# Reading the moving operand of the large products one column from each half in turn

## The chip, the core and the metric

The kernel runs on one core of a Trainium2 chip, a single program with one launch. The metric is device time in microseconds. Each of the kernel's large products is a TensorE instruction that streams a moving operand of 128 partitions x 512 columns past a stationary one of 128 x 128 and adds into an accumulator of 512 fp32 columns.

## The reference

Linear attention over q, k and v of shape (8, 8, 576, 64) gives 4608 tokens of 512 values. Two feed-forward layers of width 2048 follow, the first with ELU between its products, the second with a rational function. Some inputs are scaled by 8, weights come partly as float64 (by their bits).

```python
q_s = softmax(q, over d); k_s = softmax(k, over s)
kv = einsum('bhsd,bhse->bhde', k_s, v)
x = einsum('bhsd,bhde->bhse', q_s, kv)        # then tokens x 512
h = x @ w_in;  g = where(h > 0, h, exp(min(h, 0)) - 1);  x = g @ w_out
h = x @ w2_in
g = (a0 + a1*h + a2*h**2 + a3*h**3) / (1 + |b0|*|h| + |b1|*h**2 + 1e-6)
out = g @ w2_out
```

## The kernel before

Tokens are worked in 9 blocks of 512 (`TB`). Inside a block, position i*128 + p of a tile holds token 4p + i, since the attention loads rows four to a partition. A product in full precision is made of three TensorE products of fp32r halves: high x high, high x low, low x high. Weights lie in slots as high and low halves, inputs as tiles `xs` and `gs` (or `g`) of 128 x 2 x 512, high and low.

`plan_in` makes one tile of h (128 hidden columns x 512 tokens): for 4 pieces of the 512 inputs, three products each (lines 632 to 634), with the weights `w_in` stationary and the tokens `xs` moving, into a PSUM bank `ps`. `plan_elu` and `plan_rational` turn h into g element by element on ScalarE, VectorE and GpSimd (line 203 makes the high half, line 206 the low). `plan_out` multiplies g by `w_out` at line 673 into four accumulators `acc`: in the first layer `w_out` is stationary and the tokens g move, so the result has tokens along the columns again; in the second layer g is stationary and `w_out` moves, so the result has 128 tokens on the partitions. A tile takes 12 products in and 12 out; there are 2 layers x 9 blocks x 16 tiles, 6912 large products in all. `plan_store` copies each finished accumulator to an SBUF tile `e` (ScalarE, line 711; for the two first blocks, whose sums are made in two halves, VectorE adds at line 707) and stores it (line 715). The result's rows go out four apart, as the tokens lie.

Beside it the attention runs, one block ahead: fp32 products at lines 501 and 558 and transposes at lines 479, 486 and 547. At the start the weights of the first layer are made from float64 bits on VectorE and ScalarE (lines 317 to 362).

The order of all instructions is set by `Plan.run`: every piece of work has engines with a cost in us, what it comes after, a rank and the buffers that it takes and frees; the planner lets simulated time run and issues what can start first, lower rank first. Three large products have the cost 0.68 there (lines 645 and 683), a copy on ScalarE 0.62. Each engine works its instructions in the order issued.

Of the kernel before, what the change touches and what calls it, by code (L numbers as in the profile page):

```python
# [12 lines left out]
AF = mybir.ActivationFunctionType  # L13
ALU = mybir.AluOpType
# [4 lines left out]
P = 128  # L19
TB = 512  # L20
# [3 lines left out]
class Plan:  # L24
# [15 lines left out]
    def op(self, engines, fn, after=(), rank=0.0, take=(), free=(), extra=0.0, follow=()):  # L40
        o = dict(follow=[a for a in follow if a is not None], issued=None, engines=engines, fn=fn, after=[a for a in after if a is not None], rank=rank, take=take,
                 free=free, extra=extra, held={}, end=None, next=[], n=len(self.ops))
        waits = o["after"] + o["follow"]
        o["left"] = len(waits)
        for a in waits:
            a["next"].append(o)
        self.ops.append(o)
        return o
# [55 lines left out]
def linear_attention_elu_rational(  # L104
# [31 lines left out]
    nc = tc.nc  # L136
# [4 lines left out]
    KD = DM // P  # L141
# [13 lines left out]
    x1_d = {(j, i): dram.tile([P, TB], F32, name=f"x1_{j}_{i}") for j in range(NB) for i in range(KD)}  # L155
# [17 lines left out]
    op = plan.op  # L173

    def PE(c):
        return (("PE", c),)
# [4 lines left out]
    def DVE(c=0.75):  # L181
        return (("DVE", c),)

    def ACT(c=0.62):
        return (("ACT", c),)
# [10 lines left out]
    def f32_tile(tag, bufs, pool=None):  # L196
        return (pool or main).tile([P, TB], F32, tag=tag, name=tag, bufs=bufs)

    def bank():
        return ps_p.tile([P, TB], F32, tag="ps", name="ps")  # L200

    def copy_hi(hi, src):
        nc.scalar.activation(out=hi, in_=src, func=AF.Copy)  # L203
# [202 lines left out]
    last = {}  # L406
# [11 lines left out]
    def plan_pair(j, hp, r, gate=None):  # L418
# [58 lines left out]
        def k_maxT(e):  # L477
            b["mt"] = bank()
            nc.tensor.transpose(b["mt"][:, 0:P], b["km"].rearrange("p h d -> p (h d)"), ident)
# [17 lines left out]
        def kv_mm(e):  # L497
            pk = b["pk"] = bank()
            for i in range(NS):
                for h in range(2):  # L500
                    nc.tensor.matmul(pk[h * D:(h + 1) * D, 0:D + 1], b["ke"][:, i, h], b["vt"][:, i, h],  # L501
                                     start=(i == 0), stop=(i == NS - 1))
# [41 lines left out]
        def q_T(e):  # L544
            pt = b["pt"] = bank()
            for i in range(4):
                nc.tensor.transpose(pt[:, i * P:(i + 1) * P], b["qe"][:, i].rearrange("p h d -> p (h d)"), ident)  # L547
# [60 lines left out]
    slot_ready = {}  # L608
# [9 lines left out]
    def step_of(L, j, f):  # L618
        return place[L, j, f]

    def plan_in(t, b):
        L, j, f = t
        s = step_of(*t)

        def mm(kks):
            def fn(e):
                if 0 in kks:
                    b["h"] = bank()
                w = slot[f, 0].rearrange("p s (k c) -> p s k c", c=P)
                for kk in kks:  # L630
                    x = x_tile[L, j, kk]
                    nc.tensor.matmul(b["h"], w[:, 0, kk, :], x[:, 0], start=(kk == 0), stop=False)  # L632
                    nc.tensor.matmul(b["h"], w[:, 0, kk, :], x[:, 1], start=False, stop=False)  # L633
                    nc.tensor.matmul(b["h"], w[:, 1, kk, :], x[:, 0], start=False, stop=(kk == KD - 1))  # L634
            return fn

        parts = [(i,) for i in range(KD)] if f in (0, KF - 1) else [tuple(range(KD))]
        o = None
        for n, kks in enumerate(parts):
            free = []  # L640
            if f == KF - 1:
                free += [(x_owner[L, j, kk][0], x_owner[L, j, kk][1]) for kk in kks]
            if j == NB - 1 and n == len(parts) - 1 and f % 2:
                free.append((f"w{f // 2}_0", slot_owner[L, f, 0]))
            o = op(PE(0.68 * len(kks)), mm(kks),
                   [last.get("mm_in"), slot_ready[L, f, 0]] + [x_ready[L, j, kk] for kk in kks],
                   s, take=["bank"] if n == 0 else [], free=free,
                   follow=[x_owner[L, j, kk][1] for kk in range(KD)] if n == 0 and f == 0 else [])
            if n == 0:
                b["h_op"] = o  # L650
            last["mm_in"] = o
        in_ops[t] = o
        return o

    def plan_out(t, b):
        L, j, f = t
        halves = L == 0 and j < 2
        f0, f1 = (f - f % HALF, f - f % HALF + HALF - 1) if halves else (0, KF - 1)
        r = step_of(*t) + (1.2 if step_of(*t) < HALF else LAG[L] + 0.5)

        def mm(idx):
            def fn(e):
                for i in idx:
                    if f == f0:
                        accs[L, j, i] = acc_p.tile([P, TB], F32, tag="acc", name="acc")
                    o, g, w = accs[L, j, i], b["g"], slot[f, 1]
                    c = slice(i * P, (i + 1) * P)
                    if L == 0:
                        l3 = ((w[:, 0, c], g[:, 0]), (w[:, 0, c], g[:, 1]), (w[:, 1, c], g[:, 0]))
                    else:  # L670
                        l3 = ((g[:, 0, c], w[:, 0]), (g[:, 0, c], w[:, 1]), (g[:, 1, c], w[:, 0]))
                    for n, (lhsT, rhs) in enumerate(l3):
                        nc.tensor.matmul(o, lhsT, rhs, start=(f == f0 and n == 0), stop=(f == f1 and n == 2))  # L673
            return fn

        parts = [(i,) for i in range(4)] if f in (f0, f1) else [(0, 1, 2, 3)]
        for n, idx in enumerate(parts):
            free = []
            if n == len(parts) - 1:
                free.append(b["g_free"])  # L680
                if j == NB - 1 and f % 2:
                    free.append((f"w{f // 2}_1", slot_owner[L, f, 1]))
            o = op(PE(0.68 * len(idx)), mm(idx), [last.get("mm_out"), b["g_op"], slot_ready[L, f, 1]], r,
                   take=["acc"] * len(idx) if f == f0 else [], free=free)
            last["mm_out"] = o
            if f == f0:
                acc_op[L, j, idx[0]] = o
            if f == f1:
                plan_store(L, j, idx[0], o, r + 0.1, halves and (1 if f < HALF else 2))
        out_ops[t] = o  # L690

    accs = {}
# [3 lines left out]
    part_d = {(j, i): dram.tile([P, TB], F32, name=f"part_{j}_{i}") for j in range(2) for i in range(KD)}  # L696
    parts_stored = {}

    def plan_store(L, j, i, o, r, half):
        b = {}  # L700

        def load(e):
            b["e"] = f32_tile("e", 4)
            nc.sync.dma_start(out=b["e"], in_=part_d[j, i])

        def add(e):
            nc.vector.tensor_tensor(out=b["e"], in0=b["e"], in1=accs[L, j, i], op=ALU.add)

        def copy(e):
            b["e"] = f32_tile("e", 4)  # L710
            nc.scalar.activation(out=b["e"], in_=accs[L, j, i], func=AF.Copy)

        def store(e):
            dst = part_d[j, i] if half == 1 else x1_d[j, i] if L == 0 else out[j * TB:(j + 1) * TB, :].rearrange("(p i) c -> p i c", i=4)[:, i, :]
            nc.sync.dma_start(out=dst, in_=b["e"])

        free = [("acc", acc_op[L, j, i])]
        if half == 2:
            l = op(SP, load, [parts_stored[j, i], in_ops[0, j, KF - 1]], r - 1, take=["e"], extra=DMA)
            o1 = op(DVE(), add, [l, o], r, free=free)  # L720
        else:
            l = o1 = op(ACT(), copy, [o], r, take=["e"], free=free)
        o = op(SP, store, [o1], r, extra=DMA, free=[("e", l)])
        if half == 1:
            parts_stored[j, i] = o
        else:
            stored[L, j, i] = o
# [31 lines left out]
    def plan_rational(t):  # L759
# [49 lines left out]
        def lo(e):  # L809
            sub_lo(e, b["g"][:, 1], b["p"], b["g"][:, 0])  # L810

        o = plan_in(t, b)
        p1 = op(ACT(0.8), pstart, [o, late_op], s + 0.5, take=["p"])
        o1 = op(ACT(0.69), square, [p1], s + 0.52, take=["s"])
# [30 lines left out]
    for n in range(2 * KF):  # L845
        f, which = divmod(n, 2)
# [10 lines left out]
    for f in range(KF):  # L857
        for which in range(2):
            b = {}
            r = step_of(0, NB - 1, f) + (0.9, 3.0)[which]  # L860
# [52 lines left out]
    with tc.manual_schedule():  # L913
# [29 lines left out]
        o = op(SP, load_ab, [in_ops[0, 1, 0]], 0.0)  # L943
        op(ACT(0.2), minus_a, [o, in_ops[0, 2, 0]], 0.0)
        o = op(ACT(0.2), abs_b1, [o, in_ops[0, 2, 0]], 0.0)
        o = op(DVE(0.1), seed_b1, [o], 0.0)
        for _ in range(3):
            o = op(DVE(0.5), heron, [o], 0.0)
# [29 lines left out]
```

## Time and profile before

| | us |
|---|---|
| median of 3 runs | 1720.69 (1720.66 to 1720.9) |
| span of the profiled execution | 1719.4 |
| TensorE busy | 1676.2 |
| VectorE busy | 1065.4 |
| ScalarE busy | 1012.7 |
| GpSimd busy | 818.4 |

The profiled execution took 1719.4 us from its first to its last instruction; its own time is the span plus what lies around the span, and the median of the runs is 1.3 us over the span. The mean granted clock of TensorE is 0.992. TensorE's busy time must be read with care: a large product shows a duration of about 390 ns, but the next one starts long before it ends, so the distance of the starts is what counts. In the chain of waits each step lasts until the next one starts.

### The profile page before, as it was taken

What the parts mean: (1) busy time and instruction counts of PE and PEld (TensorE: products, weight loads), DVE (VectorE), ACT (ScalarE), POOL (GpSimd) and SP (SyncE); (2) the same over time, 40 slices, a digit from 0 to 9 for tenths busy, and PEclk for the clock granted to TensorE, in tenths of its full rate; (3) what the DMA queues carried; (4) which work ended last, traced back from release to release, by engine and by line L of the source; (5) the groups of instructions that cost most, each with busy time, mean ns of one, the idle gap of its engine ahead of it and who ended that gap; (6) DMA issues with size and microseconds to landing.
All of it is one profiled execution on the core that took longest, in us unless ns stands there. A gap on an engine that the chain in (4) does not pass through costs nothing.

```text
span 1719.4 us, 21897 instructions
## 1 busy us (share of the span) xinstructions
PE 1676.2 (97%) x7888; PEld 1363.7 (79%) x7888; DVE 1065.4 (62%) x1504; ACT 1012.7 (59%) x1696; POOL 818.4 (48%) x616
## 2 busy tenths in 40 slices
PE   4899999999999999999999999999999999999999
PEld 2577878888888887888888788888888888888887
DVE  7998646454444444422123777776868686868686
ACT  4565535454444445434456777676768686868675
POOL 2233424333333333323465756565747474747554
PEclk8899999999999999999999999999999999999999
DMA  8712433323322323210233001000101010101000
GB/s 271 231 45 81 136 114 101 90 94 90 106 72 68 114 73 117 63 43 7 92 98 104 19 15 35 13 31 2 48 1 50 1 50 0 50 0 38 0 25 25
DMA packets 110925, 112.58 MB, mean 65 GB/s; under 512 B 48864, under 2 KB 82656, under 8 KB 110816
## 3 DMA queue, kind: packets, MB, share of 16 engines
q1 hardware_dynamic: 106016, 110.00, 20.3%
q10 hardware_dynamic: 4800, 1.18, 0.3%
q8 instruction: 62, 1.02, 0.2%
q14 instruction: 47, 0.39, 0.1%
HBM read 81.79 MB, written 29.36 MB: 65 GB/s over the span
## 4 chain that ended last, share of the span: by engine, by line
PE 90%; DVE 4%; DMA 2%; ACT 1%; issue 1%; POOL 1%; SPq 0%; ACTq 0%; POOLq 0%; DVEq 0%
PE acc L673 44%; PE ps L632 14%; PE ps L634 14%; PE ps L633 14%; PE ps L558 2%; PE ps L501 1%; DMA bits<-in_moe_w_out_dram 1%; PE ps L547 1%; POOL gs L206 1%; DMA bits<-in_moe_w_in_dram 1%; DVE s L786 0%; DVE x L329 0%; DVE m L789 0%; DVE x L320 0%; DVE bits L342 0%
## 5 line engine op out<-in xcount | busy, mean ns | idle before, releaser
L632 PE MATMUL ps<-xs,w_in 128*128 128x512 f32 x1152 | 458.0, 398 | 2.8 <-DVE p L795 2.7
L634 PE MATMUL ps<-xs,w_in 128*128 128x512 f32 x1152 | 450.6, 391 | 0.0
L633 PE MATMUL ps<-xs,w_in 128*128 128x512 f32 x1152 | 449.5, 390 | 0.0
L673 PE MATMUL acc<-gs,w_out 128*128 128x512 f32 x1728 | 435.1, 397 | 4.6 <-POOL gs L206 4.6
L673 PEld LDWEIGHTS acc<-gs,w_out 128*128 128x128 f32 x1728 | 319.3, 188 | 78.1 <-POOL gs L206 7.2
L206 POOL TENSOR_TENSOR gs<-m,gs 128x512 fp32r<-128x512 f32 x124 | 168.3, 1358 | 347.0 <-ACT gs L203 290.3
L741 DVE SCALAR_TENSOR_TENSOR m<-m,ps 128x512 f32<-128x512 f32 x144 | 98.6, 685 | 268.7 <-ACT m L738 266.0
L632 PEld LDWEIGHTS ps<-xs,w_in 128*128 128x128 f32 x1152 | 217.3, 189 | 51.4 <-DVE p L795 4.1
L634 PEld LDWEIGHTS ps<-xs,w_in 128*128 128x128 f32 x1152 | 217.0, 188 | 46.5
L633 PEld LDWEIGHTS ps<-xs,w_in 128*128 128x128 f32 x1152 | 217.5, 189 | 45.0 <-issue 0.5
L777 POOL TENSOR_TENSOR s<-s,m 128x512 f32<-128x512 f32 x144 | 218.7, 1519 | 32.5 <-ACT m L766 32.5
L673 PE MATMUL acc<-w_out,g 128*128 128x512 f32 x864 | 211.6, 389 | 0.0
L673 PE MATMUL acc<-w_out,gs 128*128 128x512 f32 x864 | 210.5, 389 | 0.0
L735 ACT ACTIVATE m<-ps 128x512 f32<-128x512 f32 x144 | 85.8, 596 | 207.6 <-PE ps L634 175.3
L673 PEld LDWEIGHTS acc<-w_out,g 128*128 128x128 f32 x864 | 162.1, 188 | 33.9 <-DVE g L206 0.3
L673 PEld LDWEIGHTS acc<-w_out,gs 128*128 128x128 f32 x864 | 162.2, 188 | 33.6
L206 POOL TENSOR_TENSOR g<-p,g 128x512 fp32r<-128x512 f32 x71 | 105.1, 1481 | 171.9 <-ACT g L203 109.2
L786 DVE SCALAR_TENSOR_TENSOR s<-s,m 128x512 f32<-128x512 f32 x144 | 148.1, 1028 | 48.9 <-ACT m L783 34.5
L203 ACT ACTIVATE gs<-m 128x512 fp32r<-128x512 f32 x144 | 90.6, 629 | 148.4 <-PE acc L673 124.2
L774 ACT ACTIVATE p<-ps,a_sb 128x512 f32<-128x512 f32 x144 | 112.2, 779 | 108.3 <-PE ps L634 49.3
L792 DVE TENSOR_TENSOR p<-p,ps 128x512 f32<-128x512 f32 x144 | 98.1, 681 | 83.9 <-ACT s L770 75.2
L795 DVE SCALAR_TENSOR_TENSOR p<-p,a_sb,ps 128x512 f32<-128x512 f32 x144 | 107.3, 745 | 62.6 <-ACT m L766 62.3
(102 smaller groups left out, 2016.0 us busy)
## 6 DMA issues: line engine op xcount, KB each, us to landing
x<-e SPq DMA_DIRECT2D x36, 256.0 KB, 2.1
e<-x SPq DMA_DIRECT2D x36, 256.0 KB, 2.8
out_dram<-e SPq DMA_DIRECT2D x36, 256.0 KB, 2.6
kt<-in_k_dram SPq DMA_DIRECT2D x32, 256.0 KB, 2.8
bits<-in_moe_w_in_dram SPq DMA_DIRECT2D x16, 512.0 KB, 7.5
bits<-in_moe_w_out_dram SPq DMA_DIRECT2D x16, 512.0 KB, 7.9
st<-in_moe_w_in_dram SPq DMA_DIRECT2D x16, 512.0 KB, 4.2
w<-x SPq DMA_DIRECT2D x32, 256.0 KB, 2.0
```

The source lines that it names most:

```text
L203: nc.scalar.activation(out=hi, in_=src, func=AF.Copy)
L206: engine[e].tensor_tensor(out=lo, in0=src, in1=hi.bitcast(F32), op=ALU.subtract)
L632: nc.tensor.matmul(b["h"], w[:, 0, kk, :], x[:, 0], start=(kk == 0), stop=False)
L633: nc.tensor.matmul(b["h"], w[:, 0, kk, :], x[:, 1], start=False, stop=False)
L634: nc.tensor.matmul(b["h"], w[:, 1, kk, :], x[:, 0], start=False, stop=(kk == KD - 1))
L673: nc.tensor.matmul(o, lhsT, rhs, start=(f == f0 and n == 0), stop=(f == f1 and n == 2))
L741: nc.vector.scalar_tensor_tensor(out=b["m"], in0=b["m"], scalar=-1.0, in1=b["h"], op0=ALU.add, op1=ALU.max)
L774: nc.scalar.activation(out=b["p"], in_=b["h"], func=AF.Identity, scale=a_sb[:, 3:4], bias=a_sb[:, 2:3])
L777: engine[e].tensor_tensor(out=b["s"], in0=b["s"], in1=b["a"], op=ALU.add)
L786: nc.vector.scalar_tensor_tensor(out=b["s"], in0=b["s"], scalar=1.0 + 1e-6, in1=b["a"], op0=ALU.add, op1=ALU.mult)
L792: nc.vector.tensor_tensor(out=b["p"], in0=b["p"], in1=b["h"], op=ALU.mult)
L795: nc.vector.scalar_tensor_tensor(out=b["p"], in0=b["p"], scalar=a_sb[:, 1:2], in1=b["h"], op0=ALU.add, op1=ALU.mult)
```

## The change

All large products read the moving operand through `two`: from the 512 columns, one column of the first half and one of the second in turn (0, 256, 1, 257, ...). The accumulator is written in plain order; `turned` only gives it the same shape, so column 2c + h holds what column h*256 + c of the moving operand makes. In the first layer this order is taken twice between input and result; the copy at the end reads the accumulator through `back` (every second column, then the others) and so undoes the second of the two turns, and the first stays in the order of the tokens. In the second layer the tokens are turned once more in `plan_in`, after which they lie in their natural order; `w_out`, which moves there, is turned, and the copy turns its columns back. With natural order the result's stores write 128 neighbouring rows each. The copies' destination and the sum of line 707 are split into halves to match. The planner's cost of three large products becomes 0.65. The numbers of instructions of each engine do not change, apart from the planner's order.

```diff
@@ -199,6 +199,18 @@
     def bank():
         return ps_p.tile([P, TB], F32, tag="ps", name="ps")
 
+    def two(ap):
+        return ap.rearrange("p (h c) -> p c h", h=2)
+
+    def turned(ap):
+        return ap.rearrange("p (c h) -> p c h", h=2)
+
+    def halves_of(ap):
+        return ap.rearrange("p (h c) -> p h c", h=2)
+
+    def back(ps):
+        return ps.rearrange("p (c h) -> p h c", h=2)
+
     def copy_hi(hi, src):
         nc.scalar.activation(out=hi, in_=src, func=AF.Copy)
 
@@ -629,9 +641,10 @@
                 w = slot[f, 0].rearrange("p s (k c) -> p s k c", c=P)
                 for kk in kks:
                     x = x_tile[L, j, kk]
-                    nc.tensor.matmul(b["h"], w[:, 0, kk, :], x[:, 0], start=(kk == 0), stop=False)
-                    nc.tensor.matmul(b["h"], w[:, 0, kk, :], x[:, 1], start=False, stop=False)
-                    nc.tensor.matmul(b["h"], w[:, 1, kk, :], x[:, 0], start=False, stop=(kk == KD - 1))
+                    o = turned(b["h"])
+                    nc.tensor.matmul(o, w[:, 0, kk, :], two(x[:, 0]), start=(kk == 0), stop=False)
+                    nc.tensor.matmul(o, w[:, 0, kk, :], two(x[:, 1]), start=False, stop=False)
+                    nc.tensor.matmul(o, w[:, 1, kk, :], two(x[:, 0]), start=False, stop=(kk == KD - 1))
             return fn
 
         parts = [(i,) for i in range(KD)] if f in (0, KF - 1) else [tuple(range(KD))]
@@ -642,7 +655,7 @@
                 free += [(x_owner[L, j, kk][0], x_owner[L, j, kk][1]) for kk in kks]
             if j == NB - 1 and n == len(parts) - 1 and f % 2:
                 free.append((f"w{f // 2}_0", slot_owner[L, f, 0]))
-            o = op(PE(0.68 * len(kks)), mm(kks),
+            o = op(PE(0.65 * len(kks)), mm(kks),
                    [last.get("mm_in"), slot_ready[L, f, 0]] + [x_ready[L, j, kk] for kk in kks],
                    s, take=["bank"] if n == 0 else [], free=free,
                    follow=[x_owner[L, j, kk][1] for kk in range(KD)] if n == 0 and f == 0 else [])
@@ -670,7 +683,7 @@
                     else:
                         l3 = ((g[:, 0, c], w[:, 0]), (g[:, 0, c], w[:, 1]), (g[:, 1, c], w[:, 0]))
                     for n, (lhsT, rhs) in enumerate(l3):
-                        nc.tensor.matmul(o, lhsT, rhs, start=(f == f0 and n == 0), stop=(f == f1 and n == 2))
+                        nc.tensor.matmul(turned(o), lhsT, two(rhs), start=(f == f0 and n == 0), stop=(f == f1 and n == 2))
             return fn
 
         parts = [(i,) for i in range(4)] if f in (f0, f1) else [(0, 1, 2, 3)]
@@ -680,7 +693,7 @@
                 free.append(b["g_free"])
                 if j == NB - 1 and f % 2:
                     free.append((f"w{f // 2}_1", slot_owner[L, f, 1]))
-            o = op(PE(0.68 * len(idx)), mm(idx), [last.get("mm_out"), b["g_op"], slot_ready[L, f, 1]], r,
+            o = op(PE(0.65 * len(idx)), mm(idx), [last.get("mm_out"), b["g_op"], slot_ready[L, f, 1]], r,
                    take=["acc"] * len(idx) if f == f0 else [], free=free)
             last["mm_out"] = o
             if f == f0:
@@ -704,14 +717,15 @@
             nc.sync.dma_start(out=b["e"], in_=part_d[j, i])
 
         def add(e):
-            nc.vector.tensor_tensor(out=b["e"], in0=b["e"], in1=accs[L, j, i], op=ALU.add)
+            e = halves_of(b["e"])
+            nc.vector.tensor_tensor(out=e, in0=e, in1=back(accs[L, j, i]), op=ALU.add)
 
         def copy(e):
             b["e"] = f32_tile("e", 4)
-            nc.scalar.activation(out=b["e"], in_=accs[L, j, i], func=AF.Copy)
+            nc.scalar.activation(out=halves_of(b["e"]), in_=back(accs[L, j, i]), func=AF.Copy)
 
         def store(e):
-            dst = part_d[j, i] if half == 1 else x1_d[j, i] if L == 0 else out[j * TB:(j + 1) * TB, :].rearrange("(p i) c -> p i c", i=4)[:, i, :]
+            dst = part_d[j, i] if half == 1 else x1_d[j, i] if L == 0 else out[j * TB + i * P:j * TB + (i + 1) * P, :]
             nc.sync.dma_start(out=dst, in_=b["e"])
 
         free = [("acc", acc_op[L, j, i])]
```

The cost changes the order in several places. TensorE near 138 us of the span, in the first layer, where a long row of output products stands between two groups of input products (`km` and `top` are the attention's maxima, of which `ident` makes transposes). Before:

```order
L632 MATMUL ps<-xs,w_in 128x512
L633 MATMUL ps<-xs,w_in 128x512
L634 MATMUL ps<-xs,w_in 128x512
L673 MATMUL acc<-gs,w_out 128x512 x39
L479 MATMUL ps<-ident,km 128x128
L673 MATMUL acc<-gs,w_out 128x512 x12
```

After:

```order
L645 MATMUL ps<-xs,w_in 128x512
L646 MATMUL ps<-xs,w_in 128x512
L647 MATMUL ps<-xs,w_in 128x512
L686 MATMUL acc<-gs,w_out 128x512 x12
L491 MATMUL ps<-ident,km 128x128
L686 MATMUL acc<-gs,w_out 128x512 x36
L498 MATMUL ps<-ident,top 128x128
L686 MATMUL acc<-gs,w_out 128x512 x12
```

The first transpose moved ahead of three tiles of output products, and the second one came in before the next input products.

ScalarE at the end of a block in the second layer, with the four copies out of the accumulators (`e<-acc`) between the steps of the rational function (`m`, `s`, `p`) and the next block's halves (`xs`). Before:

```order
L711 ACTIVATE e<-acc 128x512 x2
L203 ACTIVATE xs<-e 128x512
L774 ACTIVATE p<-ps,a_sb 128x512
L780 ACTIVATE m<-s,qbias 128x512
L203 ACTIVATE g_9911<-p 128x512
L783 ACTIVATE m<-m 128x512
L770 ACTIVATE s<-ps,b_sb 128x512
L203 ACTIVATE xs<-e 128x512
L766 ACTIVATE m<-ps,b_sb 128x512
L774 ACTIVATE p<-ps,a_sb 128x512
L203 ACTIVATE xs<-e 128x512
L711 ACTIVATE e<-acc 128x512 x2
```

After:

```order
L725 ACTIVATE e<-acc 128x512
L215 ACTIVATE xs<-e 128x512
L215 ACTIVATE gs<-p 128x512
L780 ACTIVATE m<-ps,b_sb 128x512
L725 ACTIVATE e<-acc 128x512 x2
L215 ACTIVATE xs<-e 128x512
L788 ACTIVATE p<-ps,a_sb 128x512
L215 ACTIVATE g_9939<-p 128x512
L794 ACTIVATE m<-s,qbias 128x512
L784 ACTIVATE s<-ps,b_sb 128x512
L725 ACTIVATE e<-acc 128x512
```

The four copies stand one, two and one now, over about the same number of other steps. On TensorE the twelve products of the block's last tile stand there as three and nine, where before they stood as four times three with input products between.

SyncE's queue in the second layer, loads of a later block's rows (`e<-x`) and stores of the result (`out_dram<-e`). Before:

```order
L890 DMA e<-x_4_0_117 128x512
L890 DMA e<-x_4_1_118 128x512
L715 DMA out_dram<-e 128x512 x2
L890 DMA e<-x_4_2_119 128x512
L890 DMA e<-x_4_3_120 128x512
L715 DMA out_dram<-e 128x512 x2
```

After:

```order
L904 DMA e<-x_4_0_117 128x512
L904 DMA e<-x_4_1_118 128x512
L904 DMA e<-x_4_2_119 128x512
L904 DMA e<-x_4_3_120 128x512
L729 DMA out_dram<-e 128x512 x4
```

All four stores of a block moved behind all four loads.

## Rows read from the trace of the kernel before

**Rows 1.** The page, busy time, share of the span and instructions of each engine:

```profile
PE 1676.2 (97%) x7888; PEld 1363.7 (79%) x7888; DVE 1065.4 (62%) x1504; ACT 1012.7 (59%) x1696; POOL 818.4 (48%) x616
```

**Rows 2.** Stretches in us: length, busy us (instructions) per engine, granted clock, DMA:

```profile
0.00:168.00 168.00, 132.36 (x668) 99.42 (x669) 148.56 (x222) 92.22 (x141) 54.66 (x46) 0.93 0.51 158
168.00:430.00 262.00, 261.57 (x1337) 211.74 (x1336) 141.08 (x243) 121.74 (x215) 97.23 (x85) 1.00 0.34 105
...
830.00:1000.00 170.00, 167.93 (x740) 138.43 (x739) 75.70 (x91) 107.92 (x183) 104.18 (x75) 1.00 0.25 76
1000.00:1300.00 300.00, 299.23 (x1321) 247.52 (x1320) 223.22 (x274) 215.71 (x359) 182.21 (x125) 1.00 0.08 26
1300.00:1600.00 300.00, 300.00 (x1325) 248.51 (x1324) 225.03 (x280) 217.70 (x362) 184.71 (x126) 1.00 0.07 22
```

**Rows 3.** Chain of waits near 140 us: start us, us, engine, tile, line:

```profile
137.02 1.24 DVE km L475
...
138.93 3.71 POOL qt L524
...
146.37 0.84 ACT x L238
...
148.00 1.71 POOL gs L206
149.75 2.77 PE acc L673 x11
```

**Rows 4.** Chain of waits at the end of the span:

```profile
1701.34 13.79 PE acc L673 x60
...
1715.16 0.60 ACT e L711
```

**Rows 5.** Chain of waits from 1000 to 1010 us:

```profile
999.88 2.72 PE acc L673 x12
1002.60 0.23 PE ps L632
...
1003.28 2.72 PE acc L673 x12
1006.00 0.23 PE ps L632
...
1009.40 0.68 PE acc L673 x3
```

**Rows 6.** TensorE by line and shape after 168 us: count, busy us, mean ns, idle before:

```profile
L632 PE MATMUL ps<-xs,w_in 128*128 128x512 f32 x1076 | 425.6, 396 | 2.8 <-DVE p L795 2.7
L634 PE MATMUL ps<-xs,w_in 128*128 128x512 f32 x1077 | 420.1, 390 | 0.0
L633 PE MATMUL ps<-xs,w_in 128*128 128x512 f32 x1077 | 419.1, 389 | 0.0
L673 PE MATMUL acc<-gs,w_out 128*128 128x512 f32 x1545 | 386.5, 396 | 0.4 <-POOL gs L206 0.4
L673 PE MATMUL acc<-w_out,g 128*128 128x512 f32 x864 | 211.6, 389 | 0.0
L673 PE MATMUL acc<-w_out,gs 128*128 128x512 f32 x864 | 210.5, 389 | 0.0
...
L547 PE MATMUL ps<-ident,qe 128*128 128x128 f32 x108 | 16.2, 273 | 0.0
...
L558 PE MATMUL ps<-qT,kvd 128*128 128x256 f32 x16 | 4.1, 378 | 0.0
```

**Rows 7.** Timeline of TensorE: start us, us until the last ends, count:

```profile
442.50 1.02 PE L558 MATMUL ps<-qT,kvd 128*128 128x256 f32 x4
...
157.97 0.60 PE L547 MATMUL ps<-ident,qe 128*128 128x128 f32 x4
```

**Rows 8.** Groups by line and shape, whole span: count, busy us, mean ns, idle before:

```profile
L711 ACT ACTIVATE e<-acc 128x512 f32<-128x512 f32 x72 | 41.6, 594 | 28.9 <-PE acc L673 28.3
...
L475 DVE TENSOR_REDUCE km<-kt 128x128 f32<-128x640 f32 x32 | 41.4, 1295 | 2.3 <-DMA kt<-in_k_dram 2.3
...
L533 DVE TENSOR_REDUCE sm<-qe 128x8 f32<-128x512 f32 x36 | 24.6, 682 | 13.0 <-ACT qe L529 12.9
...
L707 DVE TENSOR_TENSOR e<-e,acc 128x512 f32<-128x512 f32 x8 | 5.5, 683 | 3.1 <-PE acc L673 3.1
```

**Rows 9.** DMA issues: count, KB each, median us to landing:

```profile
x<-e SPq DMA_DIRECT2D x36, 256.0 KB, 2.1
...
out_dram<-e SPq DMA_DIRECT2D x36, 256.0 KB, 2.6
```

## The prediction

> **What bounds the kernel now.** I read the page's busy times first. The line to look at is TensorE: busy 97% of a span of 1719.4 us, while VectorE, ScalarE and GpSimd stand at 62%, 59% and 48% [rows 1]. A mean hides stages, so the second view is busy time by stretch [rows 2]. Up to 168 us TensorE is busy for 132.4 us only, and VectorE for 148.6 of the 168: there the fp32 weights are still being made out of their bits, and the chain of waits near 140 us runs through VectorE, ScalarE and GpSimd lines, not through TensorE [rows 3]. [...]
>
> **The distance.** In the chain of waits a step lasts until the next one starts, so it gives the distance of the starts: 12 products of line 673 from 999.88 us on take 2.72 us, and up to 1009.40 us there are 24 of line 673 and 18 of lines 632 to 634, 42 in 9.52 us, 226.7 ns each [rows 5]. [...]
>
> [...]
>
> **The change part by part.** (1) The address order. The count of products stays at 6912, with the same weights; accumulators are still written in consecutive order. [...] I take the larger of the two overheads seen, 213.3 + 2.3 = 215.6 ns, since the transposes are nearer in kind (weights loaded for each short product). That is 11.1 ns less for each.
>
> How many of them are on the path: after 168 us there are 1076 + 1077 + 1077 + 1545 + 864 + 864 = 6503 [rows 6], so 6503 x 11.1 ns = 72.2 us. The 409 before 168 us would save 4.5 us more, which I put at nothing: their cover is VectorE's conversion of weights. If that cover were thinner than I read it, the 4.5 us come on top.
>
> [...]
>
> (2) The copies out of the accumulators. 72 copies on ScalarE (594 ns) and 8 sums on VectorE (683 ns) now read every second column [rows 8]. No row of before reads an accumulator in steps. Nearest is the reduction of line 475, which hops 64 columns between elements: 1295 / 640 = 2.02 ns an element against 682 / 512 = 1.33 for the plain one of line 533 [rows 8]. That bounds the price by 0.69 x 512 = 0.35 us a copy, 25 us of ScalarE in all, which has 82 us to spare in a stretch of 300 [rows 2]; the bound below is nothing, or a few ns less. I take nothing, since the step here is one column and not 64. On the path lies the last copy (0.35 us at most), and the freeing of accumulators where one block of 512 tokens follows another. There three products take 0.65 us and a copy 0.59, so a copy of 0.94 us would hold TensorE for up to 3 x 0.29 = 0.9 us at each of the 17 such places, 15 us at the very worst.
>
> (3) The stores. The 36 stores of the result move the same 256 KB, to 128 rows in one piece. They land in 2.6 us now, the intermediate stores, already in one piece, in 2.1 [rows 9]. Only the last is on the path: 0 to 0.5 us gained. I take 0.
>
> (4) The order of work. The planner's price of three products falls from 0.68 to 0.65, so its order moves. Near 138 us, where 39 output products run with waits in them, the attention's transposes move in among them; that is in the stretch I count at nothing. At block ends in the second layer the four copies stand closer, beside nine output products in a row, which is the place priced under (2). The four stores follow all four loads of the next block, instead of standing between them; behind them SyncE has nothing that TensorE needs soon. I take 0 for these, 3 us either way.
>
> (5) Who is next. With a distance of 215.6 a step of 24 products takes 5.17 us instead of 5.44. VectorE's 225 us of 300 become 79% of the time, ScalarE's 218 become 76% [rows 2], so TensorE stays the bound.
>
> **Sum.** The profiled execution has a span of 1719.4 us; the median of the runs is 1720.7, 1.3 us more, which I keep. 1720.7 - 72.2 = 1648.5, rounded to **1649 us**, 4.2% less.
>
> **Rivals.** *Slower: every column opens a new place in memory.* Consecutive columns now lie 1024 bytes apart. If the reader fetches a piece of several neighbouring columns at a time, each column now costs a fetch. For it speaks line 475 above, which pays 0.69 ns an element for its hops [rows 8], though it also writes 128 results instead of 8; against it, VectorE's engine is not TensorE's reader, and two streams can hold two pieces. [...]
>
> [...]
>
> [...]
>
> [...]
>
> **How the numbers follow.** Forecast 0.74. With the smaller overhead seen, 0.7 ns for 2.3, the distance is 214.0 and the time 1720.7 - 6503 x 0.0127 = 1638; with the worst of the copies and of the order, 15 and 3 us, it is 1667. Half 0.07, same 0.07, slower 0.12, the last because line 475 does show a price for hops. About 0.2%, 3.4 us, is what a measurement of this kernel can tell from no change. Faster 0.81, same 0.07, slower 0.12. The range takes in the forecast and the half case, 0.81 of the chance: 1638 to 1690.
>
> **What would show it.** In the trace of after: starts of the products 215 to 217 ns apart, TensorE still busy everywhere after some 168 us, copies of about 0.6 us, VectorE near 79% in the second layer. Wrong would be: starts still 226.7 apart (same), starts of 300 ns or more with VectorE's share falling (slower), or new idle time on TensorE that ends with a copy of line 711's kind (the copies) or with VectorE (a new bound). If the starts are right and the time is not, the early stretch has grown by what the rest saved.

## The result, and the profile after

The changed kernel takes **1658.79 us** (median of 4 runs, 1658.08 to 1661.36) against 1720.68 of the kernel before in the same sitting: ratio 0.9642, 95% interval 0.9629 to 0.9656, 3.6% faster. The forecast was 1649 us, with a range of 1638 to 1690. The gain is 61.9 us where the sum had 72.2; the profiled execution has a span of 1659.6 us, 59.8 less than before.

The page's busy times of the changed kernel (compare [rows 1]):

```profile
PE 1605.1 (97%) x7888; PEld 1379.0 (83%) x7888; DVE 1064.4 (64%) x1508; ACT 1009.0 (61%) x1694; POOL 816.3 (49%) x614
```

Its busy time by stretch, with the columns of [rows 2] (length, busy us and instructions of TensorE, of weight loads, VectorE, ScalarE and GpSimd, then granted clock, DMA share, GB/s):

```profile
0.00:172.00 172.00, 132.06 (x670) 103.72 (x671) 159.35 (x221) 90.50 (x140) 60.41 (x45) 0.91 0.49 148
...
930.00:1000.00 70.00, 70.00 (x319) 61.00 (x319) 51.39 (x67) 50.07 (x83) 40.37 (x28) 0.98 0.02 7
1000.00:1300.00 300.00, 300.00 (x1392) 262.70 (x1391) 224.30 (x292) 226.97 (x378) 190.02 (x132) 1.00 0.08 28
...
1600.00:1660.00 60.00, 52.69 (x232) 44.21 (x230) 40.40 (x52) 38.30 (x64) 30.88 (x21) 0.97 0.05 18
```

TensorE is still busy everywhere in the second layer but near its end (52.7 of the last 60 us): 300 of 300 us, with 1392 instructions where before there were 1321. The first stretch is the surprise. It is longer, TensorE does no more in it, and VectorE is busy for 159.35 us where it had 148.56 in 168 [rows 2].

The chain of waits from 1000 to 1010 us (start us, us, engine, tile, line), which answers to [rows 5]:

```profile
1002.41 0.22 PE ps L645
...
1005.00 5.18 PE acc L686 x24
```

24 products take 5.18 us, 215.8 ns each; before, 42 took 9.52 us, 226.7 each. So the distance fell by 10.9 ns. No large product here starts less than 215 ns behind the one before.

Groups of the changed kernel by line and shape, those of the copies and sums (compare [rows 8]: 594 and 683 ns), then its DMA issues (compare [rows 9]: 2.6):

```profile
L725 ACT ACTIVATE e<-acc 128x512 f32<-128x512 f32 x72 | 42.6, 595 | 51.8 <-PE acc L686 44.4 <-POOL xs L218 6.5
...
L721 DVE TENSOR_TENSOR e<-e,acc 128x512 f32<-128x512 f32 x8 | 5.4, 686 | 0.7 <-PE acc L686 0.5
```

```profile
out_dram<-e SPq DMA_DIRECT2D x36, 256.0 KB, 2.1
```

Reading every second column of an accumulator costs the copies 1 to 3 ns, and the stores land 0.5 us earlier.

**Where the gain went.** The table follows the 6912 large products by number, counted from 0 to 6911; each figure is a difference of two starts in the trace, in us. "Order" is the order of work that the planner's price of three products makes. The four columns on the right are experiments, told below. Each column is one profiled execution, and those of the changed kernel (1661.36 us) and of e4 (1654.76) were the slowest of their runs, 2.6 and 3.8 us over the medians.

| products | before | after | turned reads, old order (e1) | old reads, new order (e2) | plain early reads (e4) | plain early, price by layer (e7) |
|---|---|---|---|---|---|---|
| span's start to number 410 | 168.0 | 171.7 | 178.9 | 164.1 | 166.3 | 164.8 |
| 410 to 3456 | 759.7 | 725.9 | 727.8 | 758.5 | 724.8 | 724.7 |
| 3456 to 4000 (layers change) | 126.0 | 123.7 | 121.3 | 125.0 | 122.3 | 119.7 |
| 4000 to 6000 | 454.4 | 431.7 | 434.1 | 453.3 | 431.7 | 432.2 |
| 6000 to 6911 | 206.7 | 202.5 | 197.4 | 207.9 | 203.8 | 197.4 |

10.9 ns on the 6501 steps from number 410 on are 70.9 us. The two long stretches of after deliver theirs: 33.8 us where 3046 x 10.9 ns = 33.2, and 22.7 where 2000 x 10.9 = 21.8. What misses is the early stretch, 3.6 us longer instead of level; the change of layers, 2.3 us gained instead of 5.9; and the last 911 products, 4.1 instead of 9.9. That is 13.0 us, less 2.0 gained over the forecast in the long stretches and behind the last product: 11.1 us, and 70.9 - 59.8 = 11.1.

### The profile page after: what moved, and what is told of

It reads as the page before. It is cut to its first block, busy times and chain, and to the rows that moved or that the text cites. A ratio compares the mean times of both kernels' runs of the same rounds, so it can differ in the third digit from the quotient of the medians.

```text
span 1659.6 us, 22064 instructions
## 1 busy us (share of the span) xinstructions
PE 1605.1 (97%) x7888; PEld 1379.0 (83%) x7888; DVE 1064.4 (64%) x1508; ACT 1009.0 (61%) x1694; POOL 816.3 (49%) x614
## 4 chain that ended last, share of the span: by engine, by line
PE 83%; DVE 7%; ACT 3%; issue 2%; DMA 2%; POOL 1%; SPq 0%; POOLq 0%; ACTq 0%; DVEq 0%
PE acc L686 39%; PE ps L645 13%; PE ps L646 13%; PE ps L647 13%; PE ps L570 2%; PE ps L513 1%; PE ps L559 1%; POOL gs L218 1%; DMA bits<-in_moe_w_out_dram 1%; DVE x L341 1%; DVE bits L354 1%; ACT p L788 1%; DVE bits L350 1%; ACT s L784 1%; DVE x L332 0%
## 5 line engine op out<-in xcount | busy, mean ns | idle before, releaser
L645 PE MATMUL ps<-xs,w_in 128*128 128x512 f32 x1152 | 448.1, 389 | 9.4 <-DVE m L755 3.3
L646 PE MATMUL ps<-xs,w_in 128*128 128x512 f32 x1152 | 439.7, 382 | 0.0
L647 PE MATMUL ps<-xs,w_in 128*128 128x512 f32 x1152 | 439.4, 381 | 0.0
L686 PE MATMUL acc<-gs,w_out 128*128 128x512 f32 x1728 | 411.4, 385 | 3.2 <-POOL gs L218 3.2
L686 PEld LDWEIGHTS acc<-gs,w_out 128*128 128x128 f32 x1728 | 323.6, 190 | 53.4 <-POOL gs L218 4.5
L645 PEld LDWEIGHTS ps<-xs,w_in 128*128 128x128 f32 x1152 | 219.7, 191 | 45.1 <-DVE m L755 3.7
L647 PEld LDWEIGHTS ps<-xs,w_in 128*128 128x128 f32 x1152 | 219.6, 191 | 31.8
L646 PEld LDWEIGHTS ps<-xs,w_in 128*128 128x128 f32 x1152 | 220.0, 191 | 30.6 <-issue 0.5
L218 POOL TENSOR_TENSOR gs<-p,gs 128x512 fp32r<-128x512 f32 x72 | 115.8, 1609 | 211.5 <-issue 173.4
L686 PE MATMUL acc<-w_out,gs 128*128 128x512 f32 x864 | 201.3, 382 | 2.7 <-ACT gs L215 1.6
L686 PE MATMUL acc<-w_out,g 128*128 128x512 f32 x864 | 199.8, 379 | 0.5 <-POOL g L218 0.5
L800 DVE SCALAR_TENSOR_TENSOR s<-s,m 128x512 f32<-128x512 f32 x144 | 135.9, 944 | 24.2 <-ACT m L797 24.0
```

The lines of the kernel that those rows point to most:

```text
L218: engine[e].tensor_tensor(out=lo, in0=src, in1=hi.bitcast(F32), op=ALU.subtract)
L645: nc.tensor.matmul(o, w[:, 0, kk, :], two(x[:, 0]), start=(kk == 0), stop=False)
L646: nc.tensor.matmul(o, w[:, 0, kk, :], two(x[:, 1]), start=False, stop=False)
L647: nc.tensor.matmul(o, w[:, 1, kk, :], two(x[:, 0]), start=False, stop=(kk == KD - 1))
L686: nc.tensor.matmul(turned(o), lhsT, two(rhs), start=(f == f0 and n == 0), stop=(f == f1 and n == 2))
L800: nc.vector.scalar_tensor_tensor(out=b["s"], in0=b["s"], scalar=1.0 + 1e-6, in1=b["a"], op0=ALU.add, op1=ALU.mult)
```

## The experiments

### The order and the reads, one without the other

Two kernels, `e1_old_cost` (the changed kernel with the old price) and `e2_new_cost_old_reads` (the kernel before with the new price). The first:

```diff
-            o = op(PE(0.65 * len(kks)), mm(kks),
+            o = op(PE(0.68 * len(kks)), mm(kks),
...
-            o = op(PE(0.65 * len(idx)), mm(idx), [last.get("mm_out"), b["g_op"], slot_ready[L, f, 1]], r,
+            o = op(PE(0.68 * len(idx)), mm(idx), [last.get("mm_out"), b["g_op"], slot_ready[L, f, 1]], r,
```

> The changed kernel with the planner's cost of three large products put back from 0.65 to 0.68, so that the order of work is the old one; reads, copies and stores stay changed. Theory A (the 10 us that are missing against the forecast are lost by the new order, at the change of layers and at the end): 1649 us, within 4. Rival B (a faster TensorE meets the same chains of the other engines in any order): 1656 to 1662 us, as the changed kernel.

> The kernel before with the planner's cost put from 0.68 to 0.65 and nothing else: the new order with the old reads. Theory A: slower than before by 3 to 10 us (1724 to 1731), with TensorE waiting at the change of layers and near the end. Rival B: 1719 to 1723 us, since at a distance of 226.7 ns the other engines have time enough in either order.

Measured: e1 1664.72 us (1663.32 to 1666.74), ratio 0.9672 (0.9656 to 0.9688); e2 1715.34 us (1714.47 to 1716.47), ratio 0.9968 (0.9957 to 0.998). My first theory, that the new order had cost the missing 10 us, falls: with the old order the changed kernel is 5.9 us slower. And the new order alone, with the old reads, gains 5.4 us. Neither theory had either number. So the reads are worth 56.0 us with the old order and 56.5 with the new one, the order 5.4 to 5.9, and the reads miss some 15 of their 70.9 us.

The table shows where. Against the kernel of the same order, the turned reads make the early stretch longer by 10.9 us (168.0 to 178.9) with the old order and by 7.6 (164.1 to 171.7) with the new. The tail is another matter: with the old order the last 911 products gain 9.3 us, nearly all of their 9.9, with the new order 5.4.

### What in the reads is faster: other orders of the columns

`e3_orders` gives each block of 512 tokens another order of the moving columns, and in three blocks lets the stationary operand step as well. Its copies leave these orders in the result, and only the distances of its products are used here, not its time.

```diff
+    ORDER = {0: ("two", "two", "plain", "plain", "plain", "h16", "t8", "n64", "two"),
+             1: ("two", "plain", "evod", "h4", "t2", "t4", "t16", "n16", "n4")}
+    STEP = {(0, 3): 4, (0, 4): 2, (0, 8): 4}
...
+        m = MOVE[ORDER[L][j]]
+        if m:
+            o, rhs = o.rearrange(m[1], **m[2]), rhs.rearrange(m[0], **m[2])
+        nc.tensor.matmul(o, lhsT, rhs, **kw)
```

> The changed kernel with another order of the moving operand in each block (the copies don't restore these, so the result is another one), and in three blocks of the first layer stationary operands that step over 4 or 2 columns. Theory S (each place of memory is read at half rate, so any two places in turn do it): two halves, quarters, sixteenths and near groups of 64 and 16 columns at 215.8 ns, the even columns before the odd ones at 226.7 or more, runs of 16 from each half at 226.7. [...] Rival W (the stationary operand's reads collide with the moving one's): the plain order with a stationary step of 4 columns goes over 226.7 ns, and the halves with a step of 4 over 215.8.

The chain of waits in ten of its blocks (start us, us, engine, tile, line, count). In the order of time: stationary columns 4 apart beside plain reads; sixteen places in turn; runs of 8 columns from each half; pairs of places 64 columns apart; halves in turn with the stationary columns 4 apart; plain; all even columns, then all odd ones; quarters in turn; two columns from each half; places 16 columns apart:

```profile
402.42 2.95 PE ps L232 x12
...
652.72 5.21 PE acc L232 x12
...
784.13 2.92 PE acc L232 x12
...
872.47 2.59 PE ps L232 x12
...
963.94 2.85 PE acc L232 x12
...
1141.53 2.72 PE ps L232 x12
...
1242.29 5.44 PE ps L232 x12
...
1400.70 3.28 PE acc L232 x12
...
1509.42 4.00 PE ps L232 x12
...
1821.15 2.59 PE acc L232 x12
```

Each row is twelve products, so the distances are 246, 434, 243, 216, 238, 227, 453, 273, 333 and 216 ns. Three things follow.

- Of the 226.7 ns, 10.9 belong to the moving operand's addresses, as the prediction had it: plain reads beside the same weights show 227 again, two places in turn 216, and it doesn't matter whether the places lie 256, 64 or 16 columns apart (4 apart too: a median of 216).
- It is no matter of "more streams are better", and theory S, each place read at half rate, falls. Four places in turn take 273 ns, 1.27 times the 215.8 of two, and sixteen take 434, 2.01 times. Two columns from one place and then two from the other cost 333, runs of 4 some 250, of 16 240: all slower than plain reads and than single columns in turn.
- The even columns and then the odd ones cost 453, twice the plain 226.7. I have no rule that gives all ten numbers, and that stays open.

With the stationary columns 4 apart the products lie farther apart in both orders: 238 for 216 ns with the halves, and beside plain reads 246 in the row shown, some 237 over that block, for 227. Rival W had foreseen that, but it does not show that weight reads meet the moving reads, for the weight loads themselves take longer. Weight loads of output products, first in the first layer's plain block, then with columns 4 apart beside plain reads, then beside halves in turn (count, busy us, mean ns, idle before):

```profile
L232 PEld LDWEIGHTS acc<-gs,w_out 128*128 128x128 f32 x192 | 35.6, 188 | 7.5
...
L232 PEld LDWEIGHTS acc<-gs,w_out 128*128 128x128 f32 x177 | 41.9, 302 | 0.6
...
L232 PEld LDWEIGHTS acc<-gs,w_out 128*128 128x128 f32 x155 | 37.6, 326 | 0.2
```

At 302 and 326 ns for 188 the loads go on nearly without a pause (busy 87.1 of 90 us and 74.7 of 75 in these two blocks), so the longer distance can be theirs alone. Why they take longer stays open.

The slower rival of the prediction, a fetch for every column, does not fit these rows. One column from each half in turn never reads two neighbouring columns in a row and is the fastest, at 216 ns; the evens and then the odds never do so either and cost 453, twice the plain order.

### Who pays for it early: VectorE

In the early stretch, where the weights are made from float64 bits, some of VectorE's instructions read every second 32-bit word. To see whether TensorE's new reads lengthen them, `e4_plain_early` gives the changed kernel plain reads in the first tiles only, and `e5_turned_early_only` gives the kernel before turned reads in the first 16 tiles only, without the copies that would turn the result back.

```diff
-                    o = turned(b["h"])
-                    nc.tensor.matmul(o, w[:, 0, kk, :], two(x[:, 0]), start=(kk == 0), stop=False)
+                    o, m = (halves_of(b["h"]), halves_of) if s < 4 * HALF else (turned(b["h"]), two)
+                    nc.tensor.matmul(o, w[:, 0, kk, :], m(x[:, 0]), start=(kk == 0), stop=False)
...
-                        nc.tensor.matmul(turned(o), lhsT, two(rhs), start=(f == f0 and n == 0), stop=(f == f1 and n == 2))
+                        if step_of(*t) >= 2 * HALF:
+                            o, rhs = turned(accs[L, j, i]), two(rhs)
+                        nc.tensor.matmul(o, lhsT, rhs, start=(f == f0 and n == 0), stop=(f == f1 and n == 2))
```

> The changed kernel with the plain order of the moving operand while weights are made from bits: input products of the first two blocks in layer one (32 tiles), output products of the first 16 tiles. Tokens of these blocks are then turned once only, and the second layer stores their rows two apart. Theory C (TensorE's turned reads lengthen those VectorE instructions that step over the bits, and this stage hangs on VectorE): these instructions take their old durations again (line 342's kind 1285 ns for 1544), product 410 starts 6 to 8 us earlier, 16 tiles of input products later on cost 192 x 10.9 ns = 2.1 us: 1653 us, within 2. Rival D (the start is late because TensorE falls to half clock after its longer waits): product 410 and the time stay, 1658 to 1661.

```diff
+                    o, m = (turned(b["h"]), two) if s < 2 * HALF else (b["h"], lambda ap: ap)
...
+                        if step_of(*t) < 2 * HALF:
+                            o, rhs = turned(accs[L, j, i]), two(rhs)
```

> The kernel before with the turned order in the first 16 tiles alone (input and output products; the copies don't restore it, so the result is another one) and the old planner's cost. Theory C: the products there lie 10.9 ns nearer, and still the kernel gets slower, by 5 to 10 us (1726 to 1731), with VectorE's instructions on the bits some 20% longer. Rival D: no change or a gain, 1717 to 1721.

Measured: e4 1650.96 us (1648.72 to 1654.76), ratio 0.9584 (0.9568 to 0.96), faster than the changed kernel; e5 1732.59 us (1730.77 to 1733.31), ratio 1.0061 (1.0046 to 1.0076), slower than the kernel before. Both lie on the side of theory C, that the early reads cost time: the median is 7.8 us lower with them taken away, 11.0 higher with them put in alone. The sizes fit less well. e4 came out at the lower edge of its 1651 to 1655, with product 410 only 5.4 us earlier (171.7 to 166.3) where 6 to 8 were expected; in e7, which has the same early tiles, it is 6.9 earlier, so two executions can differ by 1.5 us there. e5 lies above its 1726 to 1731: the early stretch of its trace is 8.0 us longer (168.0 to 176.0), and another 1.6 us go at the change of layers (127.6 for 126.0), where its clock fell to half.

VectorE's groups from 90 to 165 us (count, busy us, mean ns), first of the kernel before (plain reads, old order), then of e5 (turned, old order), of e4 (plain, new order), of the changed kernel (turned, new order). `bits<-bits` and `x<-bits` read or write every second word of the bits, `x<-x` reads no bits:

```profile
L342 DVE SCALAR_TENSOR_TENSOR bits<-bits 128x1024 f32<-128x1024 uint32 x8 | 10.5, 1313 | 0.0
...
L347 DVE TENSOR_SCALAR x<-x 128x1024 int32<-128x1024 int32 x8 | 6.9, 867 | 0.0
...
L320 DVE TENSOR_SCALAR x<-bits 128x1024 int32<-128x1024 int32 x7 | 5.1, 735 | 0.0
```

```profile
L348 DVE SCALAR_TENSOR_TENSOR bits<-bits 128x1024 f32<-128x1024 uint32 x8 | 13.5, 1692 | 0.0
...
L326 DVE TENSOR_SCALAR x<-bits 128x1024 int32<-128x1024 int32 x7 | 6.9, 995 | 0.0
...
L353 DVE TENSOR_SCALAR x<-x 128x1024 int32<-128x1024 int32 x8 | 6.6, 831 | 0.0
```

```profile
L354 DVE SCALAR_TENSOR_TENSOR bits<-bits 128x1024 f32<-128x1024 uint32 x8 | 10.2, 1277 | 0.0
...
L359 DVE TENSOR_SCALAR x<-x 128x1024 int32<-128x1024 int32 x8 | 6.6, 822 | 0.0
...
L332 DVE TENSOR_SCALAR x<-bits 128x1024 int32<-128x1024 int32 x7 | 4.9, 707 | 0.0
```

```profile
L354 DVE SCALAR_TENSOR_TENSOR bits<-bits 128x1024 f32<-128x1024 uint32 x8 | 12.9, 1611 | 0.0
...
L332 DVE TENSOR_SCALAR x<-bits 128x1024 int32<-128x1024 int32 x7 | 7.2, 1045 | 0.0
...
L359 DVE TENSOR_SCALAR x<-x 128x1024 int32<-128x1024 int32 x7 | 5.0, 711 | 0.0
```

The same instruction on the bits takes 1313 and 1277 ns beside plain reads and 1692 and 1611 beside turned ones; its neighbour 735 and 707 against 995 and 1045. The instruction without bits grows in neither pair (867 and 831, 822 and 711). (Rows stand by busy time, so `x<-x` is last where the others have grown.) So the lengthening follows TensorE's order of reads, in both orders of work, and hits the instructions that step over words. The busy time of the early stretch up to product 410 says the same, e4 first, then e5:

```profile
0.00:166.30 166.30, 131.85 (x669) 99.47 (x670) 148.64 (x222) 91.33 (x140) 52.51 (x45) 0.94 0.50 154
```

```profile
0.00:176.00 176.00, 133.92 (x668) 103.77 (x669) 160.27 (x222) 90.63 (x141) 56.10 (x46) 0.90 0.49 151
```

About the same number of instructions keeps VectorE busy for 148.64 us with plain reads and 159.35 with turned ones in the new order of work, and for 148.56 [rows 2] and 160.27 in the old one: some 11 and 12 us more, of which 5.4 and 8.0 reach the start of product 410. The granted clock falls along, from 0.94 to 0.91 and from 0.93 to 0.90. Rival D, the clock alone, is out, since VectorE's own instructions grew and plain reads give the time back; how much of the delay is the lower clock that came with it was not parted.

### What the order loses at the end

`e6_plain_early_066` is e4 with the price 0.66 for 0.65, a try at the waits that remained.

```diff
-            o = op(PE(0.65 * len(kks)), mm(kks),
+            o = op(PE(0.66 * len(kks)), mm(kks),
```

> The kernel with the plain early order and the planner's cost at 0.66 for 0.65. If the waits at the change of layers and at the end (some 6 us) hang on the planner's order, 1647 to 1651; if on the lengths of the chains of the other engines, within 2 us of the same kernel at 0.65.

Measured: 1655.93 us (1655.3 to 1660.18), ratio 0.9622 (0.9608 to 0.9637), 5.0 us slower than e4 and so neither of the two. The change of layers took 120.4 us instead of 122.3, but products 410 to 2000 took 390.3 instead of 384.6, and the tail kept its waits (202.4). So a new price can move gains from one place to another.

The tail of the changed kernel, in its chain of waits:

```profile
1638.35 1.68 POOL gs L218
...
1643.81 1.32 DVE s L800
...
1645.88 0.76 DVE p L813
...
1646.72 0.64 ACT gs L215
...
1647.47 1.62 POOLq L988
...
1649.13 6.72 PE acc L686 x22
```

Ahead of its last 22 products TensorE waits for the rational function (ScalarE 1.6, GpSimd 1.0 and 0.5 us):

```profile
PE acc L686 <- ACT gs L215: 1.6, 1, 1.6
PE acc L686 <- POOL gs L218: 1.0, 1, 1.0
PE acc L686 <- POOL g L218: 0.5, 1, 0.5
```

From the first to the last of the 22 the starts then lie 301 ns apart (1649.13 to 1655.46 us; the row's 6.72 us hold the last one's own duration too), since the granted clock is at half (0.50) from 1649.5 to 1652.9 us: 21 x 0.085 = 1.8 us. With 3.1 us of waits that is 4.9 of the 5.8 missing. Before, 60 products ran there without a wait [rows 4]. The change of layers shows the same pair:

```profile
925.85 0.67 DVE p L809
...
926.65 0.76 PE ps L645
927.41 0.43 PE ps L646
```

There TensorE waits 2.85 us for VectorE (1.96 before, at the same place), and behind the wait products lie 0.43 us apart: the granted clock is at half from 925.9 to 932.7 us, where it had not fallen before. The first product behind the wait with the wait in brackets, before, then after, and the clock of the changed kernel (the column behind GpSimd's) in this stretch and in the tail's:

```profile
957.42 0.50 PE L632 MATMUL ps<-xs,w_in 128*128 128x512 f32 x1 [1.96 <-DVE p L795]
```

```profile
926.65 0.76 PE L645 MATMUL ps<-xs,w_in 128*128 128x512 f32 x1 [2.85 <-DVE p L809]
```

```profile
925.90:932.70 6.80, 6.05 (x14) 4.82 (x15) 4.92 (x7) 5.18 (x10) 5.27 (x4) 0.50 0.15 39
1649.50:1652.90 3.40, 3.40 (x10) 2.65 (x9) 0.82 (x2) 0.63 (x1) 0.00 (x0) 0.50 0.00 0
```

Since e1's tail had no wait and its order differs from the changed kernel's in the price alone, `e7_plain_early_split_cost` takes e4 and goes back to 0.68 in the second layer only:

```diff
-            o = op(PE(0.65 * len(kks)), mm(kks),
+            o = op(PE((0.65 if L == 0 else 0.68) * len(kks)), mm(kks),
```

> The kernel with plain reads in the early tiles (1650.96 us), with one number changed: the planner's price of three large products stays 0.65 in the first layer and goes back to 0.68 in the second. Theory O (the missing gain at the end of the span belongs to the order that the price of 0.65 makes in the second layer: the last 911 products took 202.5 us with 0.65 and 197.4 with 0.68, both with turned reads): the last 911 products take 197 to 199 us, the first 3456 start where they did, and the time is 1643 to 1648 us. Rival N (the waits at the end come about by chance with any order, and the old price was lucky there once): the last 911 products take 201 to 205 us and the time is 1649 to 1655 us.

Measured: **1644.74 us** (1643.53 to 1646.13), ratio 0.9558 (0.9545 to 0.9571), as theory O had it. The last 911 products take 197.4 us, the change of layers 119.7, and the first 3456 are where e4 had them (889.5 us, 891.0). Its stretch at the end has a clock of 0.99 where the changed kernel's had 0.97, and no wait of TensorE:

```profile
1600.00:1643.00 43.00, 39.11 (x179) 33.29 (x177) 28.58 (x37) 26.74 (x44) 19.44 (x14) 0.99 0.07 25
```

So the tail's loss belongs to the order that 0.65 makes in the second layer. (The whole difference to e4, 6.2 us by the medians, is less than the tail's 6.4 and the 2.6 at the change of layers, since e4's trace is of its slowest run.) This kernel beats both of the case, by 75.7 us and by some 14.

## Why the prediction was right, and where it was mis-sized

- **What bounds: right.** From about 170 us on the time is a count of products times their distance (TensorE busy for 300 of 300 us at a granted clock of 1.00 from 1000 to 1300 us; before, 299.2 [rows 2]), and the two long stretches gained 33.8 and 22.7 us where the distance gives 33.2 and 21.8.
- **(1) The distance: right, its reason only in part.** Forecast 215.6 ns, measured 215.8; 10.9 ns saved for each instead of 11.1. No run shows the 213.3 ns of the forecast's sum, nor the 2.3 and 0.7 ns taken above such a base; the runs show 226.7 ns before and 215.8 after, and starts 109 ns apart for the transposes of line 547 and 214 for the products of line 558, the last two worked out from durations whose ends the profile models [rows 6, 7]. So the close fit is partly luck. That the addresses of the moving operand decide holds (e3); my idea of why, two streams in place of one, was an estimate, and it does not explain the quarters, the sixteenths and the pairs.
- **(1) The 409 early products at nothing, with VectorE's conversion as their cover: the step that failed.** The cover was real, but I took its length as fixed. The change lengthened it by 7.6 us (new order) to 10.9 (old order), because the turned reads lengthen VectorE's stepped instructions, 1277 to 1611 ns. I had priced what the copies on ScalarE and VectorE would read, and not what runs on VectorE beside TensorE's new reads. The closing sentence of the prediction named this sign (starts right, time not), with no price for it.
- **(2) The copies: right.** 595 for 594 ns, 686 for 683; the bound of 0.35 us each was far above it.
- **(3) The stores: right.** 2.1 for 2.6 us; the end of the span behind the last product's start is 0.5 us shorter.
- **(4) The order, 0 within 3 us: mis-sized.** Alone it is worth -5.4 us (e2), -5.9 beside the new reads. It is a sum of opposite parts: the early stretch 3.9 us shorter with the old reads and 7.2 with the new, the tail 5.1 longer with the new reads (197.4 to 202.5). I had weighed three places of the order, and not the last block's end. That its gain of 5.9 us stands against the early loss is luck: with the old order the same reads give 1664.7 us (e1), 16 over the forecast.
- **(5) TensorE stays the bound: right.** VectorE stands at 224.3 of 300 us, 75% and not 79%. Some of its instructions in the second layer became shorter (line 800 takes 936 ns, the same instruction, line 786 of the kernel before, 1068); why was not tried.
- **Rivals.** *Slower* (starts of 300 ns or more) is what the changed kernel does not do, but what evens and odds or sixteen places do (453, 434). *Same* is excluded by e3's plain blocks (227 beside the same weights). *Half* (half of the 11.1 ns, 1685 us) is out: the distance fell whole, and what is missing was lost elsewhere.

Two of the three losses are shown by runs that remove them: the early reads (e4; e5 puts them in alone) and the tail (e7). The split of the tail's loss into waits and half clock was read from the trace alone. So was the change of layers: 3.6 us missing, 0.9 us more of waiting and a half clock that had not been there; with another price for the second layer it takes 119.7 us for 123.7 (e7), and no run parts the wait from the clock.

## What to carry to other kernels

Where large products wait for nothing, as here with starts 226.7 ns apart, try reading the moving operand from two places in turn, exactly two and one column each, and measure: four places (273 ns) and two columns each (333) were slower here than the plain order. Price such a change on the other engines as well: an engine that you count as cover can be lengthened by the reads of the one it covers (1277 to 1611 ns here), so compare the mean duration of its instructions, group by group, before and after. And a planner's price acts stage by stage: set it for each stage by the waits at that stage's ends.

## What the hardware showed that I had not expected

- Two places in turn take 215.8 ns for 512 columns, where consecutive columns take 10.9 ns more and four places 57.
- VectorE's instructions that step over 32-bit words take 26 to 48% longer beside these reads (1277 to 1611 ns, 707 to 1045), while one without the step does not (822 to 711).
- A half clock can follow a single wait in a stretch that is otherwise full, and the length of the wait alone does not say when. It came with 2.85 us in the changed kernel (925.9 to 932.7 us) and behind 1.94 us in e5 (966.6 to 970.0), and did not come behind 1.96 us before or 2.24 us in e1, all at the change of layers. e5's wait and clock, then e1's wait:

```profile
965.41 0.50 PE L639 MATMUL ps<-xs,w_in 128*128 128x512 f32 x1 [1.94 <-DVE p L804]
```

```profile
966.60:970.00 3.40, 3.40 (x10) 2.62 (x9) 2.64 (x4) 2.79 (x5) 3.40 (x3) 0.50 0.00 0
```

```profile
936.31 0.45 PE L645 MATMUL ps<-xs,w_in 128*128 128x512 f32 x1 [2.24 <-DVE p L809]
```
